# A fused attention, dense layer and routed-expert kernel: the gate's transposed pieces lie in an x buffer, and one more attention chunk keeps its operands in four small tiles

## The chip, the cores and the metric

One core of one Trainium2 chip runs the whole program. The time is the device time of one execution in microseconds (us). The core has five engines that run side by side: TensorE (PE, with its weight loads PEld), VectorE (DVE), ScalarE (ACT), GpSimd (POOL) and SyncE (SP), whose queue issues nearly all transfers here. Each engine takes its instructions strictly in the order in which the program was built.

## The reference

Three stages follow each other: a decayed linear attention, a dense layer with a smooth nonlinearity, and a mixture of eight experts with a fixed capacity.

```python
# attention: B,H,S,D = 4,8,768,64
state = gamma * state + k_t v_t^T ;  y_t = scale * q_t state
x = y as (3072, 512)
# dense: w_in (512, 2048), w_out (2048, 512)
h = x @ w_in ; g = h * tanh(softplus(h)) ; x = g @ w_out
# experts: w_gate (512, 8), w1 (8, 512, 1024), w2 (8, 1024, 512)
logits = x @ w_gate
# tokens are given to experts greedily by descending logit, 384 places each
out[mask_e] = relu(x[mask_e] @ w1[e]) @ w2[e]
```

## The kernel before

All large products are made of float16 pairs: a float32 array is scaled and split into a high and a low half (`split`, L209 to L229), and a product is three matmuls, high by high, high by low and low by high (`mm3`). The 3072 tokens are eight groups of 384, and a group is three chunks of 128. Group g has an attention phase (`attention`), a phase for h (`h_phase`, on PE `ph<-xt,WIN`, 192 matmuls of 128x384) and a phase for x (`x_phase`, on PE `px<-WOUT,G`, 144 matmuls of 128x512). The routing and the experts follow when all groups are done. From the third group on, h of a group and x of the group before alternate on PE in an order that is written out; before that, the build interleaves what is emitted by priority.

**The attention of a chunk.** Chunk n loads k, q and v into `ld` (one buffer), takes their sums of squares (`chunk_in`, ACT), sets scales (`chunk_scales`), and splits k, q and v into eight halves kh, kl, qh, ql, vh, vl, kkh, kkl (`att_split`); kkh and kkl are kh and kl transposed by a DMA (L366). In the trace, DVE's L229 on `ld` with `sq` makes kl, POOL's L223 on `ld` makes ql and vl. Then come the scores in two halves (L397 to L399 into `pa`, masked by DVE L400 into `amt`), the state's product (`pst`, L417 to L419) and the output (`py`, L434). After the third chunk of a group, the largest sum of squares gives one scale (L502, L202), three tiles `yh` are split from the result `yv`, and three DMA transposes (L354) put them into the group's `xt`, which has two buffers.

**Where a chunk's halves lie** is decided in `operands` (L307). Chunks 0 to 5 use the place of WOUT. Chunk 6, the first of group 2, uses two `xr` tiles (two buffers) and two `yh` tiles (three buffers). From chunk 7 on it is the upper quarter of `RAW`. Two of the raw pieces of `w_out` lie there until WOUT is split from them, and so chunk 7 waits in `attention` until `wout_split` has been emitted (the list `WO`).

**The weights.** `wout_split` splits WOUT in eight steps, the last two of them from `RAW`. `gate_setup` then multiplies `w_out` by `w_gate`, so that the logits can be taken from g. It transposes the sixteen halves of WOUT by DMA (L1054), one piece of 128x1024 each, into `yh` tiles. For each of eight pairs of pieces it issues sixteen small matmuls (L1061, L1062). `yield KN['gw']` sets how far apart the pairs are emitted. The x of group 0 runs at the same time.

```python
wv.run(h_phase(1))
need(lambda: WO)
wv.add(gate_side())
wv.run(x_phase(0))
need(lambda: G_)
```

Of the kernel before, what the change touches and what calls it, by code (L numbers as in the profile page):

```python
# [13 lines left out]
F16 = mybir.dt.float16  # L14
# [11 lines left out]
G = 384  # L26
# [72 lines left out]
def moe_kernel(ctx, tc, qkv, w_in, w_out, w_gate, w1p, w2p,  # L99
# [205 lines left out]
    prev = [None, None]  # L305

    def operands(n):  # L307
        if n == 2 * CPG:
            pairs = [wk.tile([128, ROW], F16, name="xr", tag="xr", bufs=2)[:, :2 * DM] for _ in range(2)]
            pairs += [wk.tile([128, 2 * DM], F16, name="yh", tag="yh", bufs=3) for _ in range(2)]  # L310
        else:
            v = WOF[:, n % CPG * 2048:n % CPG * 2048 + 2048] if n < 2 * CPG else RAW[:, 6144:8192]
            v = v.bitcast(F16)
            pairs = [v[:, i * 1024:i * 1024 + 1024] for i in range(4)]
        return [x.rearrange("p (n a d) -> p n a d", n=2, a=KD) for x in pairs]
# [139 lines left out]
    def attention(g):  # L455
# [23 lines left out]
            att_split(n + 1)  # L479
        for c in range(CPG):  # L480
            if g > 1:
                while n + c == 2 * CPG + 1 and not WO:
                    yield 1.0, 0.0
                att_split(n + c)
                if n + c < NT - 1:
                    chunk_in(n + c + 1)
                yield 4.0, 0.0
# [550 lines left out]
    WG = cst.tile([128, NF, 2 * E], F16, name="WG")  # L1038
    i_wg = cst.tile([128, 1], F32, name="i_wg")

    def gate_setup():

        ssg = cst.tile([128, 1], F32, name="ssg")
        A.activation(junk(KD * E), wg_raw.rearrange("p k e -> p (k e)"), AF.Square, accum_out=ssg)
        yield 4.0, 0.0
        s_gate, i_gate = pow2(total(ssg, 1), "sgate", 1)
        wgs = cst.tile([128, KD, 2 * E], F16, name="wgs")
        split(wgs[:, :, :E], wgs[:, :, E:], wg_raw, s_gate)
        pg = ps_h()[:, :NF * 2 * E].rearrange("p (f e) -> p f e", e=2 * E)
        for f2 in OI:  # L1050
            wt = []
            for a in range(2):
                w = wk.tile([128, 2 * DM], F16, name="yh", tag="yh", bufs=3).rearrange("p (j k f) -> p j k f", j=2, k=KD)
                SY.dma_start(w.rearrange("p j k f -> p (j k) f"), WOUT[:, f2, a].rearrange("p j d -> p (j d)"),  # L1054
                             transpose=True)
                wt.append(w)
            yield KN['gw'], 0.4
            for j in range(2):
                ft = 2 * f2 + j
                for k in range(KD):  # L1060
                    T.matmul(pg[:, ft, :], wt[0][:, j, k, :], wgs[:, k, :], start=k == 0, stop=False)  # L1061
                    T.matmul(pg[:, ft, :E], wt[1][:, j, k, :], wgs[:, k, :E], start=False, stop=k == KD - 1)  # L1062
# [209 lines left out]
```

## Time and profile before

| | |
|---|---|
| median of three runs | 1086.93 us (1086.38 to 1089.77) |
| the profiled execution | 1086.88 us, of which 1085.0 us from the first instruction to the last |
| mean granted TensorE clock | 0.955 of full speed |
| PE, DVE, ACT, POOL busy | 961.6, 768.9, 663.2, 407.4 us |
| instructions | 19820 |

The profiled execution lies 0.05 us under the median. Around the span lie 1.88 us. Of the page's 40 slices each is 27.1 us long; the change touches the seventh to the eleventh (163 to 298 us). "Granted clock" is a mean over a stretch: 1.00 is 2.4 GHz, 0.50 is 1.2 GHz, and other numbers are mixtures of the two.

### The profile page before, as it was taken

What the parts mean: (1) busy time and instruction counts of PE and PEld (TensorE: products, weight loads), DVE (VectorE), ACT (ScalarE), POOL (GpSimd) and SP (SyncE); (2) the same over time, 40 slices, a digit from 0 to 9 for tenths busy, and PEclk for the clock granted to TensorE, in tenths of its full rate; (3) what the DMA queues carried; (4) which work ended last, traced back from release to release, by engine and by line L of the source; (5) the groups of instructions that cost most, each with busy time, mean ns of one, the idle gap of its engine ahead of it and who ended that gap; (6) DMA issues with size and microseconds to landing.
All of it is one profiled execution on the core that took longest, in us unless ns stands there. A gap on an engine that the chain in (4) does not pass through costs nothing.

```text
span 1085.0 us, 19820 instructions
## 1 busy us (share of the span) xinstructions
PE 961.6 (89%) x7921; PEld 557.6 (51%) x7921; DVE 768.9 (71%) x1751; ACT 663.2 (61%) x1013; POOL 407.4 (38%) x292
## 2 busy tenths in 40 slices
PE   3448876987999999999999999999899999999996
PEld 2334543443655555655565655554455555545543
DVE  6799979843675866866777855567888888887341
ACT  6457876752456657577577657713367566757762
POOL 4745553561342643642653622300124412413111
PEclk9859889878999999999999999999999999999999
DMA  9551361239023023113113301015365566657420
GB/s 315 167 155 38 115 178 52 56 68 187 10 79 78 21 79 78 50 40 89 40 49 89 79 11 39 1 41 214 126 166 166 185 158 170 191 190 194 129 107 30
DMA packets 109196, 114.71 MB, mean 106 GB/s; under 512 B 92528, under 2 KB 92656, under 8 KB 107056
## 3 DMA queue, kind: packets, MB, share of 16 engines
q1 hardware_dynamic: 102720, 66.50, 24.2%
q0 software_dynamic: 6384, 46.94, 12.8%
q8 instruction: 62, 1.02, 0.4%
q14 instruction: 30, 0.25, 0.1%
HBM read 78.28 MB, written 13.91 MB: 85 GB/s over the span
## 4 chain that ended last, share of the span: by engine, by line
PE 47%; DVE 23%; issue 8%; ACT 7%; DMA 6%; POOL 3%; SPq 0%; POOLq 0%; ACTq 0%; DVEq 0%
PE ph L525 19%; PE px L525 19%; DVE WIN L229 2%; DVE WOUT L229 2%; DMA yh<-WOUT 1%; ACT junk L878 1%; DVE ld L373 1%; PE py L434 1%; DVE ld L688 1%; DVE G L966 1%; DVE RAW L571 1%; DVE RAW L555 1%; DMA RAW<-in_w1p_dram,MASK 1%; DMA ld<-in_qkv_dram 1%; DVE G L574 1%
## 5 line engine op out<-in xcount | busy, mean ns | idle before, releaser
L525 PE MATMUL ph<-xt,WIN 128*128 128x384 f16 x1728 | 328.9, 333 | 11.6 <-DVE RAW L555 4.6
L525 PE MATMUL px<-WOUT,G 128*128 128x512 f16 x1344 | 335.5, 386 | 2.9 <-DVE WOUT L229 1.5
L525 PEld LDWEIGHTS <-WIN 128*128 128x128 f16 x1920 | 186.0, 100 | 151.1 <-issue 25.4
L525 PEld LDWEIGHTS <-G 128*128 128x128 f16 x1728 | 165.1, 99 | 185.3 <-issue 14.8
L577 POOL TENSOR_TENSOR G<-RAW,G 128x1536 f16<-128x1536 f32 (+1 forms) x32 | 101.9, 3183 | 98.9 <-DVE G L574 79.4
L555 DVE TENSOR_SCALAR RAW<-ph 128x384 f32<-128x384 f32 x124 | 68.0, 550 | 45.1 <-PE ph L525 44.6
L406 POOL TENSOR_TENSOR amt<-amt 128x512 f16<-128x512 f32 x40 | 53.6, 1339 | 123.3 <-DVE amt L403 87.1
L562 ACT ACTIVATE RAW<-RAW,zt,ch 128x1536 f32<-128x1536 f32 x32 | 53.3, 1664 | 42.4 <-DVE RAW L555 38.8
L325 ACT ACTIVATE junk<-ld 128x512 bf16<-128x512 f32 x63 | 39.5, 627 | 63.3 <-DMA ld<-in_qkv_dram 62.3
L878 ACT ACTIVATE junk<-RAW 128x1024 bf16<-128x1024 f32 x64 | 67.4, 1053 | 8.6 <-DMA RAW<-in_w1p_dram,MASK 6.6
L571 DVE TENSOR_TENSOR RAW<-RAW 128x1536 f32<-128x1536 f32 (+1 forms) x33 | 56.5, 1711 | 13.6 <-ACT RAW L570 13.5
L223 POOL TENSOR_TENSOR RAW<-ld,RAW 128x512 f16<-128x512 f32 x34 | 46.5, 1383 | 43.2 <-ACT RAW L222 30.8
L966 DVE TENSOR_TENSOR G<-G,G 128x384 f16<-128x384 f32 x64 | 35.1, 551 | 33.9 <-ACT G L965 33.8
L400 DVE TENSOR_TENSOR amt<-pa,MASK 128x512 f32<-128x512 f32 x38 | 26.1, 686 | 37.5 <-PE pa L399 30.1
L986 POOL DMA_INDIRECT out_dram<-G,MASK x15 | 26.2, 1749 | 61.5 <-ACT G L985 60.3
L616 ACT ACTIVATE junk<-px 128x512 bf16<-128x512 f32 x24 | 14.0, 584 | 57.2 <-PE px L525 57.2
L570 ACT ACTIVATE RAW<-RAW 128x1536 f32<-128x1536 f32 (+1 forms) x33 | 47.7, 1445 | 0.4
L525 PEld LDWEIGHTS <-WOUT 128*128 128x128 f16 x384 | 36.3, 99 | 22.3
L563 ACT ACTIVATE RAW<-RAW 128x1536 f32<-128x1536 f32 x32 | 47.2, 1475 | 0.4
L223 POOL TENSOR_TENSOR STH<-SC,STH 64x256 f16<-64x256 f32 x34 | 29.5, 869 | 45.8 <-ACT STH L222 42.8
L525 PE MATMUL ph<-WIN,G 128*128 128x512 f16 x192 | 44.8, 379 | 1.6 <-DVE G L966 0.8
L688 DVE TENSOR_TENSOR ld<-MASK,ld 128x1536 bf16<-128x1536 bf16 (+1 forms) x35 | 44.5, 1273 | 0.5
(590 smaller groups left out, 1970.5 us busy)
## 6 DMA issues: line engine op xcount, KB each, us to landing
ld<-in_qkv_dram SPq DMA_DIRECT2D x20, 768.0 KB, 4.8
G<-in_w_in_dram SPq DMA_DIRECT2D x8, 1024.0 KB, 6.4
G<-in_w_out_dram SPq DMA_DIRECT2D x8, 1024.0 KB, 5.6
x_rows<-xr SPq DMA_DIRECT2D x25, 256.5 KB, 3.0
G<-in_qkv_dram SPq DMA_DIRECT2D x2, 768.0 KB, 6.3
g_columns<-G SPq DMA_DIRECT2D x1, 1024.0 KB, 8.4
G<-g_columns SPq DMA_DIRECT2D x1, 1024.0 KB
ld<-in_qkv_dram SPq DMA_DIRECT2D x3, 256.0 KB, 3.0
```

What stands on the lines that cost most here:

```text
L223: (V if pool in ("V", "E") else P).tensor_tensor(lo, src, hi, op=OP.subtract)
L406: (P if mode[1] == "P" else V).tensor_tensor(amh[:, j, 1], am, amh[:, j, 0], op=OP.subtract)
L525: T.matmul(p, a, b, start=i == 0, stop=i == n - 1)
L555: V.tensor_scalar(hs[:, f], p[:, :G], 1.0 / 65536.0, None, op0=OP.mult)
L562: A.activation(th, hs, AF.Tanh, scale=ch[:, q:q + 1], bias=z)
L563: A.activation(th, th, AF.Arctan, scale=-0.5, bias=0.5)
L570: A.activation(th[:, w], th[:, w], AF.Sin, scale=-2.0, bias=math.pi / 2)
L571: (V if hm[1] == 'V' else P).tensor_tensor(th[:, w], th[:, w], hs[:, w], op=OP.mult)
L577: (P if lo == 'P' else V).tensor_tensor(gb[:, 1, o], th[:, w], gb[:, 0, o], op=OP.subtract)
L688: V.tensor_tensor(out.rearrange("p t (j v) -> p t j v", v=VR), cv[:, ts, None, :].to_broadcast([128, n, J // VR, VR]), RT["jr"][:, i, :J]. ...
L878: A.activation(junk(1024), RAW[:, o:o + 1024], AF.Square, accum_out=ss[:, j:j + 1])
L966: V.tensor_tensor(hid[:, 1, f], hs, hid[:, 0, f], op=OP.subtract)
```

## The change

Three things change. `operands` gives four small tiles (two `xr`, two `yh`) to chunk 7 as well, so that chunk 8 is the first to use `RAW` and to wait for `WO`. The gate's pieces lie in three places of one `xt` buffer, the one that held the x of group 0, where they lay in three `yh` tiles that the attention also used. The scale of `w_gate` and its split (`gate_scale`: one square on ACT, one sum on PE, three small DVE instructions, a split on ACT and DVE) are emitted ahead of `wout_split`, and the pairs are emitted 4.0 apart where it was 5.15.

```diff
-KN = dict(... gw=5.15, ...)
+KN = dict(... gw=4.0, ...)
...
     def operands(n):
-        if n == 2 * CPG:
+        if n in (2 * CPG, 2 * CPG + 1):
...
-                while n + c == 2 * CPG + 1 and not WO:
+                while n + c == 2 * CPG + 2 and not WO:
...
-    def gate_setup():
-
+    def gate_scale():
         ssg = cst.tile([128, 1], F32, name="ssg")
         A.activation(junk(KD * E), wg_raw.rearrange("p k e -> p (k e)"), AF.Square, accum_out=ssg)
         yield 4.0, 0.0
-        s_gate, i_gate = pow2(total(ssg, 1), "sgate", 1)
-        wgs = cst.tile([128, KD, 2 * E], F16, name="wgs")
+        S_["gate"] = s_gate, i_gate = pow2(total(ssg, 1), "sgate", 1)
+        S_["wgs"] = wgs = cst.tile([128, KD, 2 * E], F16, name="wgs")
         split(wgs[:, :, :E], wgs[:, :, E:], wg_raw, s_gate)
+        yield 4.0, 0.0
+
+    def gate_setup():
+
+        places = wk.tile([128, 2, KD, G], F16, name="xt", tag="xt", bufs=2).rearrange("p a k t -> p (a k t)")
+        i_gate, wgs = S_["gate"][1], S_["wgs"]
+        n = 0
...
-                w = wk.tile([128, 2 * DM], F16, name="yh", tag="yh", bufs=3).rearrange("p (j k f) -> p j k f", j=2, k=KD)
+                w = places[:, n % 3 * 1024:n % 3 * 1024 + 1024].rearrange("p (j k f) -> p j k f", j=2, k=KD)
+                n += 1
...
     def wout_side():
+        yield from gate_scale()
         yield from wout_split()
         WO.append(1)
```

The build's priorities turn this into another order on each engine. It differs mainly between the end of h of group 1 and the start of h of group 2; from there on PE's order is the same. Three places follow. The gate's lines L1054, L1061 and L1062 are L1061, L1068 and L1069 in the changed kernel.

The SP queue, from the gate's first pieces on (`RAW<-RAW` and `yh<-xr` are the attention chunks' kk transposes, chunk 7's first; `yh<-WOUT` and `xt<-WOUT` the gate's pieces, `ld` the load of the next chunk, `xt<-yh` the x of group 2, `x_rows` results of group 0). Before (two more `xt<-yh` and six more pieces follow):

```order
L1054 DMA_TRANSPOSE yh<-WOUT 128x8x128 x3
L366 DMA_TRANSPOSE RAW<-RAW 128x8x128
L155 DMA ld<-in_qkv_dram 128x1536
L366 DMA_TRANSPOSE RAW<-RAW 128x8x128
L155 DMA ld<-in_qkv_dram 128x1536
L1054 DMA_TRANSPOSE yh<-WOUT 128x8x128 x6
L366 DMA_TRANSPOSE RAW<-RAW 128x8x128
L622 DMA x_rows<-xr 128x1026
L1054 DMA_TRANSPOSE yh<-WOUT 128x8x128
L155 DMA ld<-in_qkv_dram 128x1536
L354 DMA_TRANSPOSE xt<-yh 128x8x128
L622 DMA x_rows<-xr 128x1026
```

And now (the last pieces are shown, nothing of the gate follows):

```order
L1061 DMA_TRANSPOSE xt<-WOUT 128x8x128 x3
L366 DMA_TRANSPOSE yh<-xr 128x8x128
L155 DMA ld<-in_qkv_dram 128x1536
L1061 DMA_TRANSPOSE xt<-WOUT 128x8x128 x7
L366 DMA_TRANSPOSE RAW<-RAW 128x8x128
L155 DMA ld<-in_qkv_dram 128x1536
L1061 DMA_TRANSPOSE xt<-WOUT 128x8x128 x6
L366 DMA_TRANSPOSE RAW<-RAW 128x8x128
L622 DMA x_rows<-xr 128x1026
L155 DMA ld<-in_qkv_dram 128x1536
L354 DMA_TRANSPOSE xt<-yh 128x8x128 x3
L622 DMA x_rows<-xr 128x1026 x2
```

Before, three pieces stood ahead of chunk 7's transpose, none between chunks 7 and 8, six ahead of chunk 9's, and seven around and behind the x of group 2. Now seven stand between chunks 7 and 8, the other six right behind chunk 8's, and none behind the x of group 2.

DVE, in the splitting of WOUT (`WOUT<-WOUT,swq` and `WOUT<-RAW,swq` are its steps; `RAW<-ld,sq,RAW` before and `xr<-ld,sq,xr` now is chunk 7's kl). Before:

```order
L229 SCALAR_TENSOR_TENSOR WOUT<-WOUT,swq 128x1024
L226 TENSOR_SCALAR WOUT<-RAW,swq 128x1024
L555 TENSOR_SCALAR RAW<-ph 128x384
L229 SCALAR_TENSOR_TENSOR WOUT<-RAW,swq,WOUT 128x1024
L226 TENSOR_SCALAR WOUT<-RAW,swq 128x1024
L555 TENSOR_SCALAR RAW<-ph 128x384
L229 SCALAR_TENSOR_TENSOR WOUT<-RAW,swq,WOUT 128x1024
L229 SCALAR_TENSOR_TENSOR RAW<-ld,sq,RAW 128x512
L574 CAST G_68<-RAW 128x1536
L571 TENSOR_TENSOR RAW<-RAW 128x1536
L400 TENSOR_TENSOR amt<-pa,MASK 128x512
L574 CAST G_68<-RAW 128x1536
```

And now:

```order
L229 SCALAR_TENSOR_TENSOR xr<-ld,sq,xr 128x512
L229 SCALAR_TENSOR_TENSOR WOUT<-WOUT,swq 128x1024
L226 TENSOR_SCALAR WOUT<-RAW,swq 128x1024 x2
L555 TENSOR_SCALAR RAW<-ph 128x384
L229 SCALAR_TENSOR_TENSOR WOUT<-RAW,swq,WOUT 128x1024 x2
L555 TENSOR_SCALAR RAW<-ph 128x384
L400 TENSOR_TENSOR amt<-pa,MASK 128x512
L449 SCALAR_TENSOR_TENSOR SC_100<-pst,SC_100 64x256
L403 CAST amt<-amt 128x512
L449 SCALAR_TENSOR_TENSOR SC_100<-pst,SC_100 64x256
L574 CAST G_68<-RAW 128x1536
L335 COPY sqt<-pm 128x3
```

Chunk 7's kl was behind the last of the WOUT steps and is now ahead of the last five of them.

PE, at the gate's last matmuls. Before (all x matmuls of group 0 are issued by then, and h of group 2 has begun):

```order
L1061 LDWEIGHTS yh
L1061 MATMUL ph<-wgs,yh 128x16
L1062 LDWEIGHTS yh
L1062 MATMUL ph<-wgs,yh 128x8
L525 LDWEIGHTS WIN
L525 MATMUL ph<-xt,WIN 128x384
```

And now (94 of the 144 x matmuls of group 0 are issued by then, the other 50 follow, and h of group 2 begins behind them):

```order
L1068 LDWEIGHTS xt
L1068 MATMUL ph<-wgs,xt 128x16
L1069 LDWEIGHTS xt
L1069 MATMUL ph<-wgs,xt 128x8
L525 LDWEIGHTS G_67
L525 MATMUL px<-WOUT,G_67 128x512
```

The gate's end moved from behind the x of group 0 to 50 matmuls ahead of its end.

## Rows read from the trace of the kernel before

**Rows 1.** The page: busy share of PE and granted clock in 40 slices.

```profile
PE   3448876987999999999999999999899999999996
...
PEclk9859889878999999999999999999999999999999
```

**Rows 2.** Windows: busy us (x instructions) of PE, PEld, DVE, ACT, POOL; clock; DMA.

```profile
186.00:281.55 95.55, 80.04 (x634) 43.20 (x634) 53.91 (x119) 47.02 (x76) 35.29 (x23) 0.84 0.47 94
186.00:265.50 79.50, 65.54 (x430) 33.75 (x429) 46.80 (x94) 42.89 (x64) 34.14 (x22) 0.82 0.50 100
300.00:500.00 200.00, 197.15 (x1617) 115.30 (x1615) 143.46 (x280) 132.76 (x201) 89.19 (x63) 1.00 0.25 65
```

**Rows 3.** Chain that ended last, 241 to 273 us: start, us, what.

```profile
241.72 3.30 DMA yh<-WOUT
...
269.75 3.06 DMA yh<-WOUT
```

**Rows 4.** Everything that writes or reads the tiles yh, 180 to 280 us.

```profile
L1054 SPq DMA_TRANSPOSE yh<-WOUT x16: 1232/1242/1290, 186.0 to 269.8; - x16
...
  ACT yh L228: 6.7, 2
...
DMA to landing us min/median/max: 3.1/3.3/6.2
```

**Rows 5.** Timeline of DVE: start, us, instruction, [idle before].

```profile
198.82 0.74 DVE L226 TENSOR_SCALAR WOUT<-RAW,swq 128x1024 f16<-128x1024 f32 x1
...
202.98 0.55 DVE L555 TENSOR_SCALAR RAW<-ph 128x384 f32<-128x384 f32 x1
203.44 1.27 DVE L229 SCALAR_TENSOR_TENSOR WOUT<-RAW,swq,WOUT 128x1024 f16<-128x1024 f32 x1
204.64 1.65 DVE L229 SCALAR_TENSOR_TENSOR RAW<-ld,sq,RAW 128x512 f16<-128x512 f32 x1
...
210.30 3.25 DVE L574 CAST G<-RAW 128x1536 f16<-128x1536 f32 x1
...
224.11 0.14 DVE L192 TENSOR_SCALAR sgatea<-tot 128x1 int32<-128x1 int32 x1
...
226.26 0.74 DVE L229 SCALAR_TENSOR_TENSOR RAW<-ld,sq,RAW 128x512 f16<-128x512 f32 x1
226.93 0.38 DVE L229 SCALAR_TENSOR_TENSOR wgs<-wg_raw,sgate,wgs 128x32 f16<-128x32 f32 x1
227.23 0.95 DVE L574 CAST G<-RAW 128x1536 f16<-128x1536 f32 x1
```

**Rows 6.** Timeline of PE.

```profile
198.50 4.06 PE L525 MATMUL ph<-xt,WIN 128*128 128x384 f16 x24
...
214.36 4.46 PE L525 MATMUL px<-WOUT,G 128*128 128x512 f16 x10
...
239.77 0.60 PE L434 MATMUL py<-RAW,amt 128*128 128x64 f16 x12
...
240.43 0.28 PE L434 MATMUL py<-RAW,amt 128*128 128x64 f16 x4
...
244.45 0.32 PE L202 MATMUL pm<-identf,m 128*128 128x128 f32 x1 [1.71 <-DVE st L195]
...
255.03 6.42 PE L525 MATMUL px<-WOUT,G 128*128 128x512 f16 x29
...
281.55 1.03 PE L525 MATMUL px<-WOUT,G 128*128 128x512 f16 x4
```

**Rows 7.** PE's instructions by line and shape, 276 to 290 us: busy us, mean ns.

```profile
L591 PE MATMUL pm<-WG,G 128*128 128x16 f16 x96 | 5.1, 169 | 0.0
```

**Rows 8.** Timeline of SP's queue: the x of group 2.

```profile
256.72 3.56 SPq L354 DMA_TRANSPOSE xt<-yh  x2
```

**Rows 9.** Windows, as in group 2: a stretch in the early stage, and one behind pauses.

```profile
85.00:110.00 25.00, 19.84 (x170) 12.58 (x169) 23.85 (x54) 18.79 (x25) 15.02 (x11) 1.00 0.11 27
230.00:235.00 5.00, 5.00 (x39) 3.16 (x38) 0.93 (x2) 0.00 (x0) 3.35 (x2) 0.50 0.50 157
```

More of the change, by code (lines that the diff above doesn't have):

```diff
@@ new lines @@
+KN = dict(ea=1, sc=1, pw=4, le=0.0, hl=['P', 'P'], cs=['V', 'V', 'V', 'V', 'V', 'V', 'V'], cc=['V', 'V', 'V', 'V', 'V', 'V', 'V', 'V', 'V'], lo=['c0', 'g', 'c1', 'm', 'c2', 's', 'wg', 'w0', 'w1', 'w2'], ga=['', 'V'], rs=[[-0.63, 0.3, -1.2, 0.0, 0.24, 0.0, 0.09, 0.0, 0.21, 0.0, 0.0, -4.24], [2.1, 0.09, 2.19, 0.0, 0.58, 0.15, 0.18, 0.15, 0.26, 0.26, 1.46, -4.41], [0.26, 0.0, 1.32, 0.2, 0.33, 0.0, -0.3, 0.0, 0.09, -0.12, 0.3, -3.18], [0.56, 0.0, 0.38, 0.0, 0.15, 0.0, 1.42, -0.11, 1.26, -1.47, 0.03, -5.34], [0.67, 0.0, 0.31, 0.24, 0.89, 0.0, 0.15, -0.22, 0.0, 0.0, 2.24, -7.15], [-1.04, -2.35, 0.04, -0.29, 0.13, -0.18, -1.58, -0.4, 0.45, 0.03, 3.56, -5.57], [0.45, 0.54, 0.45, 0.0, 1.18, 0.0, 1.11, -0.55, -0.61, -0.05, 2.65, -6.07], [-0.15, 0.0, -0.75, 0.0, 0.0, 0.0, 0.0, -0.3, 0.0, 0.0, 0.28, -7.01]], fs=[[0.0, 0.0, -3.96, -1.22], [-0.75, 0.0, 1.32, 0.16], [0.0, 0.0, -2.08, 0.13], [0.0, -1.13, 0.71, 0.36], [0.0, 0.0, 0.0, -0.56], [0.38, 0.75, 0.13, 0.04], [0.0, 0.38, 0.2, 0.69], [0.0, -1.5, 2.89, 0.29]], av=[5.75, 5.75, 2.0, 4.0], a2=[1.3, 2.2, 4.3], a1=[0.1, 1.0, 0.85], ao=[3.5, 3.5, 3.35], wv=[8.5, 0.5, 1.0, 4.5], ov=5.0, an=[3.0, 3.15, 3.6], qm=['P0', 'VP', 'VP', 'PH', 'P1', 'VV', 'VP'], vm=['P0', 'VP', 'VP', 'VP', 'VP', 'P0', 'VP'], km=['A', 'H', 0, 0, 0, 0, 0], am=['AP', 'AP', 'AP', 'AV', 'AP', 'AV', 'VP'], ss=['V', 'P', 'P', 'P', 'P', 'P', 'P'], sm=['P', 'V', 'V', 'P', 'E', 'D', 'P'], ym=[0, 0, 0], hm=['VVVP', 'VVAV', 'VVVP', 'VVVP', 'AVVP', 'VVVP', 'VVVP', 'VVVP', 'VVVP'], ci=['AP'] * 8, co=['AP'] * 8, wa=[15, 12, 8, -1, 7, 16], cp=[0, 100, 0, 100], np=0, yp=[0, 2000], op=[0, 0, 200, 0, 50, 1000], xp=[0, 0, 0, 0, 0, 0], ld=[0, 1, 2, 3, 4], wj=[4, 4, 4], fw=[13.5, 18.5, 14, 16, 14, 16], qs=1.0, tw=3.0, sw=1.5, po=[[0] * 8] * 4, sl=[0, 0, 0.7], rw=[4.9, 2.5, 1.55, 1.7, 1.7], pn=0.5, lw=14.0, gx=9.0, g0=[0.5, 2.2, 1.5], tk=2.75, st=[16.0, 21.0, 20.0, 23.5], wi=['H', 'A', 0, 0, 2, 0, 0, 0], wo=['H', 'H', 0, 0, 0, 0, 'H', 0], tp=[], gw=4.0, nw=1.0, cw=0, sp=50, ap=1000, wp=None, ip=None)
```

1 line of the change is left out of this document (removed).

## The prediction

> **What bounds the kernel now.** I read the page first, by slices. From the eleventh slice to the end PE is busy nine tenths or more in nearly every slice; in the first ten it isn't, and its clock falls with it [rows 1]. The windows say the same: between 300 and 500 us PE works 197.15 of 200 us at clock 1.00, while between 186.00 and 281.55 us it has 634 matmuls in 95.55 us at a mean clock of 0.84 [rows 2]. What a stage costs behind 300 us is PE's own work. What it costs ahead of that is waiting, and the change lies there.
>
> I take 281.55 us as the mark. There PE issues the first four x matmuls of group 1 [rows 6], the first place from which PE's order is the same in both kernels. A shift of this mark is a shift of the end, if nothing later has slack against it; PE without pauses from 300 us on leaves none.
>
> How much could the stretch give? At full clock an x matmul takes 6.42/29 = 0.221 us and an h matmul 4.06/24 = 0.169 [rows 6]; a logits matmul takes 5.1/192 = 0.027, since rows with another line of as many matmuls lie in the same 5.1 us [rows 7]. The stretch has 144 x (31.8), 100 h (16.9), 128 gate and 96 logits matmuls (6.0), and 166 smaller ones of the attention and of sums, which at the 0.60/12 = 0.05 us of an output matmul [rows 6] make some 8. That is 63 us of 95.5; 32 us are pauses and low clock.
>
> Where the pauses are is what the chain of waits shows: from 241.72 to 272.8 us it holds five times `DMA yh<-WOUT`, 3.06 to 3.30 us each and some 16 us together; the first and the last are shown [rows 3]. These are the gate's pieces. PE stands still before a gate matmul, the piece is in flight, and the piece could not be issued earlier because its `yh` tile was still read, or because SP's queue stood behind another transpose. One DMA transpose takes SP 1.24 us and lands 3.3 us after its issue (3.1 to 6.2), and ACT waited 6.7 us for a gate matmul before it could write the x of group 2 into `yh` [rows 4].
>
> **The change, part by part.** I follow two lines up to the mark, the attention's and the gate's.
>
> *The attention.* Chunk 7's kl was made at 204.64 us, behind five last steps of WOUT and two evictions of h; it ended at 206.29 [rows 5]. Now it stands ahead of all seven. The five steps are three of 1.27 and two of 0.74, or 5.3 us; the evictions are two of 0.55 [rows 5], or 1.1. Its own 1.65 stood beside POOL work; alone it takes 0.74, as chunk 8's does [rows 5]. So it ends at 204.64 - 6.4 + 0.74 = 199.0, 7.3 us earlier. From this kl to chunk 8's (227.00) the steps are the same as before: 20.7 us. Chunk 8's kl then ends at 219.8. The scores and the output of chunk 8 took until 240.71, and the maximum started at 244.45 [rows 6]. That is 17.45 us behind the kl, so 237.2 now. From the maximum on, the three `yh` had to wait for gate matmuls [rows 4]; that wait goes. The scale takes about 1.5 us (an estimate from some ten steps of 0.14 like the one in [rows 5]); then come a high half and three low halves of 0.74 each, the size of a kl, the last transpose's 1.24 and its landing within 3.3: the x of group 2 is there at about 246. Before, only the issue of its last two transposes ended at 260.28 [rows 8].
>
> *The gate.* Three places stay three, so a pair of pieces can't follow the pair before it faster than a landing and its sixteen matmuls: 3.3 + 0.4 = 3.7 us. The first pair has landed long before PE comes to it, which is behind chunk 7's kk transpose: 199.0 + 3.3, and then `pst` and what stands ahead of it on PE: about 204.6. Seven more pairs alone would end at 230.5. But in PE's order the fourth pair stands behind chunk 7's output, the fifth among chunk 8's scores, and on SP the last six pieces stand behind chunk 8's transpose and one load. With chunk 8's kl at 219.8 the fifth pair ends near 227 (kl, scores in alternation with gate matmuls, and their halves), and three more pairs with their x matmuls between end at about 240.
>
> *The end of the stretch.* Behind the gate stand 50 x matmuls: 50 x 0.221 = 11.05, until 251. The x of group 2 is there by then. Up to the mark follow 52 h matmuls, 96 logits and 12 scores: 8.8 + 2.6 + 0.6 = 12.0. The mark comes at 263.0, which is 18.5 us earlier, if PE has its full clock.
>
> *The clock.* It had a mean of 0.82 between 186 and 265.5 us [rows 2], and 0.50, the lower level of 1.2 GHz, between 230 and 235, where PE was busy in all 5 us and had paused before [rows 9]. PE's own work on these two lines is the 11 us of x and some 6 us of scores, outputs and x matmuls between. At 0.82 that is 17/0.82 = 20.7: 3.7 us more. The Trainium skill (TensorE: Matmul & The Clock Gate, Part 1: The HAM clock gate) says that the lower level is PE's default and that activity releases it; by that rule alone every run behind a pause would begin at the lower level, the 50 x matmuls too, which is the fourth case below. The row agrees in that a busy stretch behind pauses stood at 0.50.
>
> *The gate's scale, moved ahead.* Its instructions are the same; on DVE the split takes 0.38 us and four small ones 0.14 each [rows 5], 0.9 to 1.0 us together. It left a place where DVE waited and goes to one between 85 and 110 us where DVE is busy 23.85 of 25 us [rows 9] and is waited for: +1.0 us. If its cover is there after all, nothing; if the new order in that stretch costs a little elsewhere, 2. I take 1.0.
>
> *At nothing:* the sixteen transposes themselves (as many as before, the same size); chunk 7's split, whose instructions only write elsewhere; the wait of chunk 8 for WOUT, since WOUT's last step (204.64 before, some 206 now) is over long before chunk 8's scales are; the `xt` buffer, whose next owner is group 3; the `xr` tiles, which x of group 0 needs for its first result only when chunk 7 is done. If that cover were gone, x of group 0 would stand still after its second bank.
>
> *The sum.* 281.55 - 263.0 = 18.5; less 3.7 for the clock, less 1.0 for the scale: 13.8 us. The profiled execution took 1086.88, 0.05 under the median: 1073.1 us, and to the median the same.
>
> **The rivals.**
>
> *More is won (1066).* Chunk 8's kl comes a little sooner, since the 20.7 us held two casts beside POOL work (3.25 us for what takes 0.95 alone [rows 5]), and the slow clock falls into pauses where it costs nothing. Then the kl is at 217.7 and the mark at 260.9, and neither 3.7 nor 1.0 is lost: 20.6 us, 1066.2. For it: ACT, DVE and POOL set most of both lines. Against it: the clock was low in nearly every loose slice.
>
> *The casts are caught again (1077.5).* Of the same two casts, both now stand between chunk 7's masks and chunk 8's kl, next to POOL's work on chunk 7's `amt` and on g. If both take 3.25 and the sums beside them as much longer, chunk 8's kl comes 4.6 us later, at 224.4, and by the gate's line so does the mark: 13.8 - 4.6 = 9.2. The Trainium skill (SBUF — State Buffer, Who interferes with whom) has this as a lock that VectorE's casts and GpSimd share and that the first to come holds for its whole instruction. The rows agree with it as far as 3.25 beside 0.95 can.
>
> *No change (1086).* PE runs all 17 us of work on the path at 1.2 GHz, as in 214.36 to 218.82, where ten x matmuls took 4.46 [rows 6], twice the 0.221. That is +17 where I took 3.7: 13.8 - 13.3 = 0.5. Against it: even the loosest window before had 0.82.
>
> *Slower (1093).* The gate's pieces now follow each other more densely, among the attention's transposes. If they land like the slowest of before, in 6.2 us [rows 4], a pair takes 6.6: seven take 46.2, to 250.8, and with the 9.5 us of other PE work between them 260.3. Fifty x matmuls later it is 271.4, the mark is at 283.4, and with clock and scale 288: 6.5 us later than before, 1093. It decides from 5.3 us a landing on: 244.7 + 7 x 5.3 is 281.8. For it: PE can't pass the gate, so each late piece stops the x matmuls. Against it: the median of the landings is 3.3, and the five on the chain took 3.06 to 3.30 [rows 3].
>
> **How the numbers follow.** The forecast gets 0.54 (own range 1069 to 1076), more won 0.17, the casts 0.18, no change 0.06, slower 0.05. The range of 8 in 10 runs from 1065 to 1081: it holds the first three cases with the bounds of clock (0 to 11 us on the 50 x matmuls) and scale (0 to 2), and leaves out the last two. About 0.3%, 3.3 us, is what a measurement of this kernel can tell from no change. Faster: 0.89, same 0.06, slower 0.05.
>
> **What would show it right or wrong.** In the profile after: chunk 7's kl on DVE before 200.5 us; chunk 8's near 220; gate matmuls over at about 240, with no `DMA xt<-WOUT` piece on the chain behind that; the 50 x matmuls in one run that ends near 251 to 255; the first four x matmuls of group 1 at 265 to 270; from there on the same distance to the end as before, 803 us. Wrong would be: a chain that still holds pieces up to the start of h of group 2; a landing of 5 us or more; a clock near 0.5 between 240 and 252; a distance from mark to end that grew by more than 3 us; or a stage before 186 us that came out more than 2 us longer.

## The result, and the profile after

The changed kernel took 1078.19 us (median of seven runs, 1075.38 to 1084.19), the kernel before 1087.51 (seven runs beside it, 1086.38 to 1089.77). The ratio is 0.9911, 95% interval 0.9887 to 0.9936. The profiled execution took 1078.19 us with a span of 1076.4. The forecast was 1073.0, its range 1065 to 1081.

The page, PE and the granted clock by slices, answers to [rows 1]. The tenth slice (244 to 271 us before, 242 to 269 now) has filled up, from 7 to 9, and the clock of the ninth and the tenth went from 7 and 8 to 8 and 9.

```profile
PE   3348777889999999999999999999899999999996
...
PEclk9958988989999999999999999999899999999999
```

Windows as in [rows 2], now up to the mark, up to the end of x of group 0, and of the 50 x matmuls alone (the ratio behind POOL's busy time is the clock):

```profile
186.00:273.31 87.31, 74.48 (x643) 40.56 (x641) 62.59 (x124) 46.96 (x74) 37.14 (x24) 0.92 0.48 103
186.00:260.90 74.90, 62.21 (x481) 32.35 (x479) 56.36 (x101) 42.97 (x62) 35.98 (x23) 0.91 0.55 117
248.00:261.00 13.00, 13.00 (x67) 5.83 (x68) 4.79 (x19) 3.09 (x6) 0.43 (x1) 0.87 0.71 167
```

The mark, the first four x matmuls of group 1, stands at 273.31 us: 8.2 earlier than 281.55, where 18.5 less 4.7 was forecast. From the mark to the end it is 803.1 us (803.4 before): nothing behind it changed.

The timeline of DVE answers to [rows 5] (start, us, instruction). The first row is chunk 7's kl, the last is chunk 8's.

```profile
199.93 0.74 DVE L229 SCALAR_TENSOR_TENSOR xr<-ld,sq,xr 128x512 f16<-128x512 f32 x1
...
214.80 1.75 DVE L571 TENSOR_TENSOR RAW<-RAW 128x1536 f32<-128x1536 f32 x1
216.47 3.06 DVE L195 TENSOR_SCALAR sq<-sqa 128x3 int32<-128x3 int32 x1
219.45 0.15 DVE L196 TENSOR_SCALAR sq<-sqa 128x3 int32<-128x3 int32 x1
...
222.08 0.95 DVE L574 CAST G<-RAW 128x1536 f16<-128x1536 f32 x1
...
223.02 0.74 DVE L373 SCALAR_TENSOR_TENSOR ld<-ld,sq,GV 128x512 f32<-128x512 f32 x1
223.68 3.58 DVE L229 SCALAR_TENSOR_TENSOR RAW<-ld,sq,RAW 128x512 f16<-128x512 f32 x1
```

And POOL beside it:

```profile
214.85 4.65 POOL L577 TENSOR_TENSOR G<-RAW,G 128x1536 f16<-128x1536 f32 x1
...
223.11 3.61 POOL L577 TENSOR_TENSOR G<-RAW,G 128x1536 f16<-128x1536 f32 x1 [0.97 <-DVE sq L339]
226.67 1.61 POOL L223 TENSOR_TENSOR RAW<-ld,RAW 128x512 f16<-128x512 f32 x1
```

Read the two together. POOL's L577 makes the low half of g. The first starts at 214.85, while DVE's L571 runs until 216.55, and ends at 219.50. DVE's next instruction has three elements in a row, 0.15 us like its neighbour; it takes 3.06 and ends at 219.53. The second L577 ends at 226.72, and chunk 8's kl, 0.74 us when nothing stands beside it, takes 3.58 and ends at 227.26. POOL's split for chunk 8 (the third row) waits behind the second L577 as well. Chunk 7's kl thus came 5.6 us earlier than before, chunk 8's not at all (227.01 before).

Where the lead was lost is seen from L335 on, with which DVE takes over the sums of chunk 8. Before:

```profile
221.31 0.16 DVE L335 COPY sqt<-pm 128x3 f32<-128x3 f32 x1 [2.17 <-PE pm L333]
```

And now:

```profile
214.06 0.16 DVE L335 COPY sqt<-pm 128x3 f32<-128x3 f32 x1 [0.56 <-PE pm L333]
```

The sums came 7.2 us earlier. From there to the end of chunk 8's kl it took 5.7 us before and 13.2 now, 7.5 more. Of these, 2.9 and 2.8 are the two instructions above. Another 0.95 is L338 on two elements a row, which took 1.10 and ended (222.15) with POOL's L406 (222.14). The rest is order: a mask, its cast and a cast of g now stand in between.

The chain of waits answers to [rows 3] (start, us, what). The L577 stands on it; two pieces of the gate are left, then the 50 x matmuls.

```profile
223.12 3.60 POOL G L577
226.72 1.57 POOL RAW L223
...
239.28 3.23 DMA xt<-WOUT
...
243.10 4.82 DMA xt<-WOUT
...
248.64 12.48 PE px L525 x50
```

SP's queue answers to [rows 8]. The seven pieces leave the queue at 227.53, just before chunk 8's transpose, and the x of group 2 is issued behind the gate's end (248.6), not behind pieces.

```profile
208.55 18.98 SPq L1061 DMA_TRANSPOSE xt<-WOUT  x7
227.62 1.29 SPq L366 DMA_TRANSPOSE RAW<-RAW  x1
...
230.33 14.00 SPq L1061 DMA_TRANSPOSE xt<-WOUT  x6
...
251.72 4.06 SPq L354 DMA_TRANSPOSE xt<-yh  x3
```

### The profile page after: what moved, and what is told of

The parts are those of the page before. It is cut to its first block, busy times and chain, and to the rows that moved or that the text cites. A ratio compares the mean times of both kernels' runs of the same rounds, so it can differ in the third digit from the quotient of the medians.

```text
span 1076.4 us, 19805 instructions
## 1 busy us (share of the span) xinstructions
PE 956.7 (89%) x7921; PEld 555.5 (52%) x7921; DVE 777.5 (72%) x1751; ACT 661.9 (61%) x1013; POOL 408.9 (38%) x292
## 4 chain that ended last, share of the span: by engine, by line
PE 47%; DVE 15%; ACT 6%; issue 6%; DMA 3%; POOL 2%; POOLq 0%; SPq 0%; ACTq 0%; DVEq 0%
PE px L525 21%; PE ph L525 19%; DVE WIN L229 2%; DVE WOUT L229 2%; ACT junk L878 2%; DVE ld L688 2%; PE py L434 1%; DVE G L966 1%; DMA RAW<-in_w1p_dram,MASK 1%; DVE RAW L571 1%; DVE ld L373 1%; PE pa L397 1%; DVE sq L338 1%; DMA xt<-WOUT 1%; POOL amt L406 1%
## 5 line engine op out<-in xcount | busy, mean ns | idle before, releaser
L525 PE MATMUL ph<-xt,WIN 128*128 128x384 f16 x1728 | 330.9, 334 | 15.4 <-DVE RAW L555 7.5
L577 POOL TENSOR_TENSOR G<-RAW,G 128x1536 f16<-128x1536 f32 (+1 forms) x32 | 102.4, 3200 | 98.4 <-DVE G L574 77.8
L406 POOL TENSOR_TENSOR amt<-amt 128x512 f16<-128x512 f32 x40 | 54.0, 1349 | 122.5 <-DVE amt L403 114.3
L571 DVE TENSOR_TENSOR RAW<-RAW 128x1536 f32<-128x1536 f32 (+1 forms) x33 | 56.8, 1722 | 13.6 <-ACT RAW L570 13.5
L223 POOL TENSOR_TENSOR RAW<-ld,RAW 128x512 f16<-128x512 f32 x32 | 43.0, 1356 | 34.1 <-ACT RAW L222 29.1
L400 DVE TENSOR_TENSOR amt<-pa,MASK 128x512 f32<-128x512 f32 x38 | 26.1, 686 | 32.5 <-PE pa L399 28.5
```

Source lines behind the costliest of these rows:

```text
L223: (V if pool in ("V", "E") else P).tensor_tensor(lo, src, hi, op=OP.subtract)
L406: (P if mode[1] == "P" else V).tensor_tensor(amh[:, j, 1], am, amh[:, j, 0], op=OP.subtract)
L525: T.matmul(p, a, b, start=i == 0, stop=i == n - 1)
L571: (V if hm[1] == 'V' else P).tensor_tensor(th[:, w], th[:, w], hs[:, w], op=OP.mult)
L577: (P if lo == 'P' else V).tensor_tensor(gb[:, 1, o], th[:, w], gb[:, 0, o], op=OP.subtract)
```

## The experiments

Two questions were open: which of the three edits makes the gain, and what cost 7.5 us at chunk 8's kl. The four kernels below "changed" ran on one chip, the next seven on a second and the last on a third, each time beside the kernel before. Times in us of the profiled executions: "kl 7" and "kl 8" are the ends of these two instructions, "gate" the start of the last gate matmul.

| kernel | ratio to before (95%) | kl 7 | kl 8 | gate | mark |
|---|---|---|---|---|---|
| before | 1 | 206.28 | 227.01 | 273.22 | 281.55 |
| changed | 0.9911 (0.9887 to 0.9936) | 200.66 | 227.27 | 248.47 | 273.31 |
| places_only | 1.0004 (0.9984 to 1.0023) | 206.09 | 226.82 | 276.01 | 282.83 |
| chunk7_only | 1.0087 (1.0070 to 1.0105) | 198.33 | 224.65 | 282.54 | 281.75 |
| scale_only | 0.9983 (0.9967 to 0.9999) | 206.99 | 226.57 | 266.38 | 276.98 |
| scale_back | 1.0057 (1.0035 to 1.0079) | 199.13 | 223.77 | 279.17 | 275.32 |
| changed, again | 0.9931 (0.9916 to 0.9947) | 202.01 | 226.93 | 248.00 | 271.18 |
| low_dve5 | 0.9874 (0.9856 to 0.9893) | 201.59 | 221.74 | 245.15 | 268.22 |
| low_dve67 | 0.9933 (0.9915 to 0.9952) | 202.05 | 226.69 | 251.38 | 274.56 |
| four_places | 0.9920 (0.9904 to 0.9936) | 200.97 | 226.84 | 238.10 | 271.18 |
| scale_back_free | 1.0046 (1.0030 to 1.0061) | 197.90 | 224.19 | 279.87 | 275.83 |
| before_low5 | 1.0002 (0.9991 to 1.0013) | 204.88 | 227.51 | 272.29 | 280.62 |
| low_dve5_four | 0.9956 (0.9944 to 0.9968) | 199.78 | 225.43 | 239.30 | 272.94 |
| low_dve567 | 0.9901 (0.9875 to 0.9927) | 202.23 | 222.34 | 243.66 | 268.89 |

On the other chips it took 807 to 811 us from the mark to the end where the gate was over ahead of the mark by 6 us or more; on the first it was 803. So marks are compared as they stand, times only by their ratios. One execution of each kernel was profiled, and it need not be a typical one: that of chunk7_only took 1110.26 us where the median of its seven is 1102.20, that of "changed, again" 1081.82 where the median of its five is 1085.23. The two marks of the changed kernel lie 2.1 us apart, so a difference of that size between two kernels says little by itself.

### One edit at a time

Theory G held that the gate's places make the gain, theory A that the earlier chunk 7 does.

**places_only**: the kernel before with the pieces in `xt`, nothing else.

```diff
+        places = wk.tile([128, 2, KD, G], F16, name="xt", tag="xt", bufs=2).rearrange(...)
...
-                w = wk.tile([128, 2 * DM], F16, name="yh", tag="yh", bufs=3).rearrange(...)
+                w = places[:, n % 3 * 1024:n % 3 * 1024 + 1024].rearrange(...)
...
```

> Of the change only the gate's places: the sixteen pieces lie in the xt buffer, chunk 7 stays in RAW behind the list WO, the scale stays inside the gate. Theory G (the time came from the gate's pieces, which no longer wait for yh tiles or keep the x of group 2 waiting for them): chunk 7's and 8's kl end as before (206 and 227 us), the x of group 2 is in place some 6 us earlier, the mark (first four x matmuls of group 1) at 273 to 276, 1079 to 1082 us. Theory A (it came from the earlier chunk 7, which the gate's places only made room for): the mark within 2 us of 281.5, 1086 to 1089 us.

Nothing moved: the pieces still come around and behind the x of group 2, and PE waited 5.3 us for `xt<-WOUT`, in four waits. Free places alone bring no piece forward if the gate starts at 230 us. Theory G alone falls.

**chunk7_only**: the kernel before with chunk 7's operands in small tiles.

```diff
-        if n == 2 * CPG:
+        if n in (2 * CPG, 2 * CPG + 1):
...
-                while n + c == 2 * CPG + 1 and not WO:
+                while n + c == 2 * CPG + 2 and not WO:
```

> Of the change only chunk 7's operands in four small tiles and the wait moved to chunk 8; the gate's pieces stay in yh tiles. Theory G: the pieces still come late, with waits of about 3.3 us each behind the x of group 0, so the mark is at 278 to 282 and the time 1084 to 1088 us. Theory A: chunk 7's kl at 199, and the mark at 272 to 275, 1078 to 1081 us.

The kl came at 198.33 and h of group 2 at 260.18 (265.77 before), yet the kernel is 0.9% slower. The build now puts the gate's first matmul at 240.87 (230.72 before), behind the earlier attention, and its end at 282.54, behind the mark. Theory A alone falls too.

**scale_only**: the kernel before with `gate_scale` ahead of `wout_split`, `gw` unchanged.

```diff
...
     def wout_side():
+        yield from gate_scale()
         yield from wout_split()
```

> Of the change only the scale of w_gate and its split ahead of the splitting of WOUT; pieces in yh, chunk 7 in RAW. Theory G: the early stage gets 1 to 2 us longer (h of group 1 starts at 141 to 142.5 where it was 139.99), but the first pairs of the gate come before chunk 7's scores, so that fewer pieces are left behind the x of group 0: mark at 277 to 281, 1083 to 1088 us. Theory A: only the loss, 1088 to 1089.5 us.

The gate starts at 202.82 and ends 7 us earlier, in spite of the `yh` tiles; the mark is 4.6 us earlier. The price is seen at the start of h of group 1: 143.00 us where it was 139.99. The ratio is just under 1.

**scale_back**: the changed kernel with `gate_scale` back inside the gate.

```diff
     def wout_side():
-        yield from gate_scale()
         yield from wout_split()
...
+        yield from gate_scale()
         yield from gate_setup()
```

> The whole change with the scale put back inside the gate, its parts otherwise as after. If the moved scale is a plain cost in the early stage, as the prediction priced it, this gains 1 to 2 us on the changed kernel: 1076 to 1077.5, with h of group 1 starting at 140. Rival: the early scale is what lets the first five pairs of the gate run beside chunk 7 and 8; without it the pairs move behind the x of group 0 and their waits of 3 us come back among the h matmuls of group 2: 1080 to 1085 us.

The whole gain is gone, and more: the moved scale, which I booked as a cost of 1.0 us, lets the gate start at 207.6 and not at 240. So no edit alone gives the gain (scale_only comes nearest, 0.2%), and neither do the other two together without the scale. The two pairs that hold the scale were not run. Here, though, chunk 8's kl, its maximum (240.85) and h of group 2 (253.94) are all earlier than in the changed kernel, and the mark is only 2 us later than its 273.31. The loss lies behind the mark: from there to the maximum of group 3 it takes 65.8 us, before and in the changed kernel 55.6. PE's timeline in scale_back:

```profile
279.19 1.44 PE L525 MATMUL ph<-xt,WIN 128*128 128x384 f16 x4
280.68 0.59 PE L185 MATMUL pm<-ssg,onesf 128*128 128x1 f32 x2
284.34 0.17 PE L591 MATMUL pm<-WG,G 128*128 128x16 f16 x1 [3.07 <-DVE WG L229]
```

And the window from there on, with the clock behind POOL's busy time (in the 5 us ahead of it PE was busy 3.34 us, at a clock of 0.84):

```profile
280.32:290.00 9.68, 5.95 (x186) 5.49 (x186) 5.49 (x13) 4.37 (x11) 3.81 (x2) 0.50 0.01 3
```

**scale_back_free**: is it the wait for the split of WG? Here, in scale_back, the logits of group 0 are multiplied with another, earlier tile, so their values are not those of the reference.

```diff
+                    wg = WG[:, ft] if g else S_["wgs"][:, ft % KD]
-                    T.matmul(p[:, c, :], gb[:, 0, ft, c * C:(c + 1) * C], WG[:, ft, :],
+                    T.matmul(p[:, c, :], gb[:, 0, ft, c * C:(c + 1) * C], wg,
...
```

> The changed kernel with the gate's scale back inside the gate (as scale_back), and the logits of group 0 multiplied with wgs, the split w_gate, in place of WG: their values are other ones, their matmuls are as many, of the same size and at the same place of TensorE's order. Theory W (a gate that ends near the mark puts what comes behind it, the sum, the scale and the split of WG, onto TensorE ahead of the logits): in scale_back TensorE stood still from 280.7 to 287.7 us, and from the mark to the maximum of group 3 it took 65.8 us where the kernel before and the changed one take 55.6. Without it 58 to 60 us are left, since the last gate pieces still come behind the mark; 6 to 8 us less in all, ratio to before 0.998 to 1.000 (scale_back: 1.0057). Rival (the late pieces themselves cost it): 64 us or more from mark to maximum, ratio above 1.003.

The expectation misread the pause: PE stood still for 3.07 us there, and in what I took for the rest of it the logits ran at the lower clock. And theory W falls: 65.4 us from mark to maximum, the ratio unchanged within the intervals. Without WG the pause was still 1.70, `[1.70 <-DVE tot L187]`: the logits also need the place of the sum ahead of them, which DVE read behind a slow L571. What the trace of scale_back adds up to is pauses of 5.4 us behind the mark (0.7 in the changed kernel), 9.68 us at 0.50 with 5.95 of work in them, which is 3.0 more than at full clock, and 96 logits matmuls that stood ahead of the mark before, 2.6 by [rows 7]: 10.3 in all, close to the 10.2 by which 65.8 exceeds 55.6. This is a sum over one trace; no run takes its terms apart.

### What held chunk 8's kl

Theory L: POOL's L577 holds up DVE's instructions that stand beside it. Rival P: the three places and SP's queue set the gate's line, whatever the kl does. Each experiment changes one to three letters in the table that gives this subtraction to POOL or DVE, by quarters of h, or the places.

**changed, again**, the control. 

> The changed kernel itself, as the control for the three others on this chip. Both theories: 0.991 of the kernel before (0.988 to 0.994), chunk 8's kl over at 227.3 us, the last gate matmul at 248.5, the mark at 273.3.

As expected up to the gate; the mark is 2.1 us earlier than in the first profile, 1.7 of it since the 50 x matmuls took 10.82 us, not 12.48.

**low_dve5**: the second quarter of group 1 on DVE.

```diff
-hm=[..., 'AVVP', 'VVVP', 'VVVP', 'VVVP', 'VVVP']
+hm=[..., 'AVVP', 'VVVV', 'VVVP', 'VVVP', 'VVVP']
```

> The changed kernel with the low half of g of group 1's second quarter (L577) made by VectorE, not GpSimd; the third quarter's L577 then stands behind chunk 8's ql and vl on GpSimd. Theory L (GpSimd's L577 holds up VectorE): in the changed kernel two instructions of VectorE end where an L577 of GpSimd ends, a three-element one of 3.06 us at 219.53 (L577 214.85 + 4.65 = 219.50) and chunk 8's kl of 3.58 at 227.26 (223.11 + 3.61 = 226.72). Both go, 2.9 + 2.8 us, and one subtraction of 1.65 (an estimate from L571's 1.75 of the same size) comes onto VectorE: kl over at 223.2, and with it chunk 8's transpose on SP, the scores and the last six pieces: the mark at 269.2, 4.1 us ahead of the control's, ratio to before 0.987. Rival P (the three places and SP's queue set the gate's line, whatever the kl does): the kl comes earlier, the last gate matmul stays within 1 us of 248.5 and the mark within 1 us of 273.3. Rival W (other instructions are held up in their place): kl not before 226, mark unchanged.

DVE in low_dve5, the subtraction, the three-element instruction and chunk 8's kl:

```profile
214.06 1.75 DVE L577 TENSOR_TENSOR G<-RAW,G 128x1536 f16<-128x1536 f32 x1
215.73 0.69 DVE L195 TENSOR_SCALAR sq<-sqa 128x3 int32<-128x3 int32 x1
...
220.10 1.63 DVE L229 SCALAR_TENSOR_TENSOR RAW<-ld,sq,RAW 128x512 f16<-128x512 f32 x1
```

And POOL:

```profile
214.09 2.30 POOL L441 TENSOR_TENSOR SC<-SC,GS 128x256 f32<-128x256 f32 x1
...
225.33 3.21 POOL L577 TENSOR_TENSOR G<-RAW,G 128x1536 f16<-128x1536 f32 x1 [0.90 <-DVE G L574]
```

Theory L holds: kl at 221.74, 5.2 us earlier than in the control, the mark 3.0 earlier at 268.22, and the ratio 0.9874 beside the control's 0.9931, with intervals apart. It has the lowest ratio found and is faster than both kernels. The other direction shows too: L441, 0.71 us alone, took 2.30 beside DVE's 1.75.

Why 5.2 us at the kl gave 3.0 at the mark is seen in part on SP's queue:

```profile
207.80 15.36 SPq L1061 DMA_TRANSPOSE xt<-WOUT  x7
223.25 1.29 SPq L366 DMA_TRANSPOSE RAW<-RAW  x1
```

The seven pieces hold the queue until 223.16, 1.4 us past the kl, so that chunk 8's transpose goes 4.0 us earlier than in the control (227.29). In that rival P has a part. And behind the kl, DVE waited 4.10 us for POOL's L406, which stood behind the L577 of 225.33.

**low_dve67**: the third and the fourth quarter on DVE, the second on POOL.

```diff
-hm=[..., 'AVVP', 'VVVP', 'VVVP', 'VVVP', 'VVVP']
+hm=[..., 'AVVP', 'VVVP', 'VVVV', 'VVVV', 'VVVP']
```

> The changed kernel with L577 of the third and fourth quarter of group 1 on VectorE; the second quarter's stays on GpSimd. Theory L: the three-element instruction is still held up (about 3 us, over when L577 is over), chunk 8's kl is not: 0.74 us, over at 227.3 - 2.8 = 224.4; GpSimd's ql of chunk 8 no longer stands behind L577. The two subtractions stand behind the kl on VectorE and take back up to 3.3 us, as far as chunk 8's masks wait for them. Mark at 270.5 to 273, ratio to before 0.988 to 0.991. Rival P: kl earlier, mark unchanged. Rival W: another instruction ahead of the kl takes over 2 us, kl at 227 as before.

DVE's timeline in low_dve67, the two instructions in question:

```profile
217.85 3.06 DVE L195 TENSOR_SCALAR sq<-sqa 128x3 int32<-128x3 int32 x1
...
225.06 1.64 DVE L229 SCALAR_TENSOR_TENSOR RAW<-ld,sq,RAW 128x512 f16<-128x512 f32 x1
```

POOL's timeline, the L577 of the second quarter:

```profile
216.24 4.64 POOL L577 TENSOR_TENSOR G<-RAW,G 128x1536 f16<-128x1536 f32 x1
```

The three-element instruction is held up again and ends (220.91) with L577 (220.88); the kl is held up 0.9 us, not 2.8. From L574 to the kl's end it takes 13.4 us, 15.4 in the control. This much is theory L. But all of it began 1.7 us later than in the control (its L574 at 213.27, there at 211.54), and the kl (226.69), the mark and the ratio lie outside what was expected. SP's queue adds to it:

```profile
209.94 18.97 SPq L1061 DMA_TRANSPOSE xt<-WOUT  x7
229.00 1.30 SPq L366 DMA_TRANSPOSE RAW<-RAW  x1
```

The pieces hold chunk 8's transpose until 229.00, 1.7 us later than in the control, though the kl was over 0.2 earlier. The ratio is the control's: no gain.

**four_places**: a fourth place for pieces, a `yh` tile.

```diff
+        more = wk.tile([128, 2 * DM], F16, name="yh", tag="yh", bufs=3)
...
-                w = places[:, n % 3 * 1024:n % 3 * 1024 + 1024].rearrange(...)
+                w = more if n % 4 == 3 else places[:, n % 4 * 1024:n % 4 * 1024 + 1024]
...
```

> The changed kernel with a fourth place for the gate's pieces, a third yh tile beside the three in the x buffer. Theory P: the pairs come one behind the other because a piece can go only when the piece three before it has been read; the last two pieces (239.28 and 243.10, 3.23 and 4.82 us on the chain) hold up the maximum behind them on TensorE and the 50 x matmuls. With four, the gate is over at about 240, the maximum at 240 to 242, the x of group 2 in place by 252, the mark at 267 to 268: 5 to 6 us ahead of the control's, ratio to before 0.985 to 0.987; chunk 8's kl stays at 227.3. Theory L alone (chunk 8's kl and its scores set both lines): the gate is over earlier, the maximum stays within 1.5 us of 248.1, the mark within 2 of 273.3. It can lose, too: if the fourth piece, in a yh tile, is read late, the x of group 2 waits for that tile, as in the kernel before.

The gate is over 10 us earlier, and the mark stands still: as the account of the mark, rival P falls. The maximum came 1.5 us earlier (246.18), and that was lost to the clock: the 50 x matmuls took 12.49 us, 10.82 in the control. One window of the control:

```profile
246.00:251.00 5.00, 3.51 (x30) 1.89 (x31) 3.69 (x19) 3.65 (x9) 2.10 (x3) 1.00 0.77 175
```

The same window with four places:

```profile
246.00:251.00 5.00, 4.82 (x15) 1.95 (x16) 4.33 (x19) 3.51 (x7) 0.86 (x2) 0.66 0.86 215
```

Before it, from 236 to 246, PE was busy 9.04 us in the control and 7.65 with four places.

Chunk 8's kl stands alone here (0.74 us), and still it ends at 226.84, as in the control. The L577 have caught others ahead of it. DVE's timeline in four_places:

```profile
213.98 3.06 DVE L192 TENSOR_SCALAR sqa<-sqt 128x3 int32<-128x3 int32 x1
...
221.79 3.05 DVE L338 TENSOR_TENSOR sq<-sq 128x2 f32<-128x2 f32 x1
```

And POOL's:

```profile
213.85 3.16 POOL L577 TENSOR_TENSOR G<-RAW,G 128x1536 f16<-128x1536 f32 x1
...
221.29 3.54 POOL L577 TENSOR_TENSOR G<-RAW,G 128x1536 f16<-128x1536 f32 x1 [0.90 <-DVE G L574]
```

The two L577 end at 217.01 and 224.83, the two instructions of DVE at 217.04 and 224.84.

**before_low5**: the one-letter diff of low_dve5, in the kernel before.

> The kernel before, with L577 of group 1's second quarter on VectorE. Theory L says what it did behind the change (4 to 6 us) is worth nothing here, since the gate's pieces in yh tiles set the end of the stretch: chunk 8's kl comes 1 to 3 us earlier than 227.0, the gate is over at 273 as before, the mark within 1 us of 281.5, ratio 0.998 to 1.001. Rival (GpSimd's work beside VectorE costs its time wherever it stands, also ahead of this stretch): the mark 3 us or more earlier, ratio 0.996 or less.

The time is unchanged, as expected, but chunk 8's kl did not come earlier either (227.51). So this run doesn't show that an earlier kl would be worth nothing there; it shows that the letter is worth nothing without the change.

**low_dve5_four**: the diffs of low_dve5 and of four_places together.

> The changed kernel with both edits, L577 of the second quarter on VectorE and a fourth place for the gate's pieces. With four places alone the gate was over at 238.3, 10 us earlier than in the control, and the maximum came only 1.5 us earlier (246.2), 19.3 us behind chunk 8's kl: the attention sets it. If the attention sets it by the kl (theory L), the kl at 221.7 puts the maximum at 241, the x of group 2 in place at 251.5 and the mark at 264 to 265, 4 us ahead of low_dve5's, ratio 0.983 to 0.985. If it is set by VectorE's work for chunk 9 that stands between the outputs of chunk 8 and the maximum, the maximum stays at 245 to 246, the mark at 268 and the ratio at 0.987. Pauses may cost up to 1.7 us more: the 50 x matmuls behind the maximum took 12.49 us with four places, where the clock was 0.66 between 246 and 251 us, and 10.82 in the control, where it was 1.00.

Neither number came: the kl is at 225.43, the maximum at 249.38, the mark at 272.94. The reason is theory L itself. With the gate's matmuls elsewhere, the third quarter's L577 fell ahead of the kl again, and the fourth's beside the next chunk's scale. DVE's timeline in low_dve5_four:

```profile
221.89 3.54 DVE L229 SCALAR_TENSOR_TENSOR RAW<-ld,sq,RAW 128x512 f16<-128x512 f32 x1
...
241.40 2.90 DVE L192 TENSOR_SCALAR sqa<-sqt 128x3 int32<-128x3 int32 x1
```

And POOL's:

```profile
221.26 3.62 POOL L577 TENSOR_TENSOR G<-RAW,G 128x1536 f16<-128x1536 f32 x1 [3.44 <-DVE sq L339]
...
241.18 3.10 POOL L577 TENSOR_TENSOR G<-RAW,G 128x1536 f16<-128x1536 f32 x1 [0.90 <-DVE G L574]
```

221.26 + 3.62 = 224.88, and the kl ends 0.55 later; 241.18 + 3.10 = 244.28, and the three-element L192 ends at 244.30.

**low_dve567**: all three quarters on DVE.

```diff
-hm=[..., 'AVVP', 'VVVP', 'VVVP', 'VVVP', 'VVVP']
+hm=[..., 'AVVP', 'VVVV', 'VVVV', 'VVVV', 'VVVP']
```

> The changed kernel with L577 of the second, third and fourth quarter of group 1 on VectorE; none of them is left on GpSimd. In low_dve5 the third quarter's L577 stood on GpSimd from 225.33 to 228.54 ahead of chunk 8's first L406, for which VectorE waited 4.10 us, and the fourth's, at 236.89, ended with a three-element instruction of VectorE that took 1.95 us. Theory L: both go; two subtractions of 1.75 come onto VectorE, where 4.1 and 2.1 us of waiting stand behind the kl. The kl stays at 221.7; chunk 8's output, the seventh gate pair and all behind it come 1.2 to 2.9 us earlier, the mark at 265.3 to 267.0, ratio to before 0.985 to 0.987. Rival: the subtractions cost VectorE what GpSimd's gave back, mark at 268 to 269, ratio 0.987 to 0.989. With four places and the same VectorE edit the third quarter's L577 fell ahead of chunk 8's ql again and took back the gain; here it can't.

The rival's mark came, but not for its reason. No L577 was left on POOL for DVE to wait for, and the maximum came at 240.15, 5.9 us earlier than in low_dve5; so the two subtractions did not cost DVE what they gave back. But the mark stayed at 268.89. Of the two lines the pieces now end last, as the chain of waits of this kernel has it:

```profile
225.23 4.46 DMA xt<-WOUT
...
234.58 3.23 DMA xt<-WOUT
...
238.40 4.85 DMA xt<-WOUT
```

By this chain rival P would be right for this kernel. Yet the gate, too, was over 1.5 us earlier than in low_dve5, and that was lost behind it: PE waited 0.86 us for a result of group 0, `[0.86 <-DVE xr L229]`, and its clock was low, after 6.62 us of work in the 10 from 236 to 246:

```profile
245.00:252.00 7.00, 7.00 (x27) 2.87 (x27) 4.49 (x19) 2.83 (x5) 1.01 (x1) 0.81 0.86 214
```

All three quarters on DVE with four places would be next; it was not run.

## Why the prediction was right, and where it was off

Right in direction and range, and in the main mechanism: the pieces left the stretch behind the x of group 2, the mark moved, and what lies behind it did not. By the steps:

- *Chunk 7's kl*: 199.0 forecast, 200.66 measured; the start of h of group 1 had slipped by 2.3 us.
- *"From this kl to chunk 8's (227.00) the steps are the same as before: 20.7 us."* **This step failed.** It took 26.6 (24.9 in the control). The steps were not the same: the five steps of WOUT that chunk 7's kl had passed now stand behind it. No cost of that shows, since chunk 8's sums came 7.2 us earlier all the same. What cost was the neighbours: two L577 of POOL now fell on a three-element instruction (2.9 us too long) and on the kl (2.8). low_dve5, low_dve67 and low_dve5_four show this cause by taking it away, halving it and bringing it back; in low_dve5 the two kls lie 20.2 apart. Chunk 8's kl was 7.5 us late by it and by the 1.7 above.
- *17.45 us from this kl to the maximum*: 20.9. In low_dve567, with no L577 on POOL, it was 17.8.
- *The gate's end at about 240*: 248.6. The kl's delay is 7.5, but it doesn't pass on one to one: in low_dve5 the kl is 5.2 us earlier than in the control and the gate 2.9, and with four places the gate is 9.9 earlier at the same kl. So the three places hold the gate as well.
- *50 x matmuls in 11.05 us*: 12.48 at a clock of 0.87. So the clock, for which 3.7 was set aside, cost 1.4 here; the control shows 10.82 at full clock.
- *12.0 us from there to the mark*: 12.4.
- *The scale, 1.0 us*: mis-sized. h of group 1 starts at 139.99 to 140.74 in the six kernels with the scale in the gate, at 141.94 to 143.91 in the eight with it ahead: 1.2 to 3.9 us, 2.3 in the changed kernel. And it is no plain cost: without it the gate starts 32 us later.
- *The sum*: the mark came 10.3 us behind 263.0. The 4.7 set aside for clock and scale cover part; 5.6 are left. 1073.1 + 5.6 less the 0.3 by which the rest was shorter is 1078.4; measured, 1078.19. That the time lies in the range is in part luck: clock and scale took some 3.1 of the 4.7 (1.4 and, at chunk 7's kl, 1.7), and the rest went to a delay that it wasn't meant for.
- *The signs*: of those that were to show it right, the kls, the gate's end, the end of the x matmuls (260.9) and the mark all came late, and pieces were left on the chain behind 240. Of those that were to show it wrong, two came: a landing of 6.1 us, and an early stage 2.3 us longer.

The rival "the casts are caught again" gave 1077.5 and was nearest. Its place was right (POOL beside DVE ahead of chunk 8's kl), its victims were not: the casts took 1.62 and 0.95 us. That its time came nearest is luck as well: of its 4.6 us the casts could give 1.3, since the 20.7 us of before already hold one of 3.25 and one of 1.91, and L571 took 1.75 as before. The Trainium skill (SBUF — State Buffer, Who interferes with whom) has it that the one that comes second waits for the first one's whole instruction, and that order, not shape, decides who waits. The rows agree to 0.1 us for the three-element instruction: L577 waits for L571, runs 2.95 us, and that instruction ends 0.03 us behind it; the kl ends 0.54 behind its L577. "More is won", "no change" and "slower" did not come. For "no change" the work on the path had to run at 1.2 GHz throughout: the 50 x matmuls stood at 0.87, and in the control, 0.5 us behind a pause of 1.95, at 1.00. For "slower", the slowest landing in the new trace is 6.1 us, but not on the path; the two on the path took 3.23 and 4.82.

## What to carry to other kernels

When an edit moves work, its durations don't move with it: list the long instructions of POOL that will stand beside it on DVE, and put down as a risk that a short instruction on the path takes the whole rest of the long one. Not every one is caught: in the kernel before, the mask L400, which reads `pa`, took 0.68 us (209.70) beside an L577 that ran until 212.73. Edits that free a place, an operand and a scale can each be worth next to nothing or a loss and pay when they come together, since what counts is where the build then puts the waiting matmuls. After each gain look again at which line ends last: here it was the gate, then gate and attention close together (248.6 and 248.4 in the changed kernel), the attention in low_dve5 and four_places, and the gate again in low_dve567.

## What was not expected of the hardware

- A 128x3 instruction of DVE took 3.06 us beside a 128x1536 subtraction of POOL, twenty times its 0.15. Such instructions (L192, L195) took 2.90 to 3.06 beside an L577 in seven of the kernels, and one of 128x2 (L338) took 3.05 in four_places.
- The same program ran its 50 x matmuls in 12.48 us in one execution and 10.82 in another, at clocks of 0.87 and 1.00 in that stretch. Ahead of it, from 243 to 248 us, PE had been busy 2.92 us in the first and 3.05 in the second.
- Behind the mark, kernels with one and the same order on PE there took 803 us on one chip and 807 to 811 on three others.
